# Three instead of two of eight value parts weighted on VectorE, ahead of the keys' last sum, in a two-layer decode kernel

## The chip, the cores and the metric

The kernel runs on one core of a Trainium2 chip. The metric is the device time of one execution in microseconds, as the median of several runs. Before the change it is 2681.38 us (three runs, 2681.13 to 2682.27).

## What is computed

Two decoder layers, each a block of attention over a cache and a gated MLP, for two sequences (B = 2) with one new token each. Both layers use the same weights and the same caches. All numbers are 32-bit floats.

```python
B, Sq, D = 2, 1, 576
H, Sk, Dh = 32, 8192, 128        # k_cache and v_cache: (B, H, Sk, Dh)
Dm, Df = 576, 4608

def _A_ref(x, k_cache, v_cache, wq, wo):
    q = (x @ wq).reshape(B, Sq, H, Dh).transpose(0, 2, 1, 3)
    scores = jnp.einsum("bhqd,bhkd->bhqk", q, k_cache) * (Dh ** -0.5)
    p = _softmax(scores, axis=-1)
    o = jnp.einsum("bhqk,bhkd->bhqd", p, v_cache)
    return o.transpose(0, 2, 1, 3).reshape(B, Sq, H * Dh) @ wo

def _B_ref(x, w_gate, w_up, w_down):
    h = _gelu(jnp.einsum("bsd,df->bsf", x, w_gate)) * jnp.einsum("bsd,df->bsf", x, w_up)
    return jnp.einsum("bsf,fd->bsd", h, w_down)

x = A_x
x = x + _A_ref(_layernorm(x), A_k_cache, A_v_cache, A_wq, A_wo)
x = x + _B_ref(_layernorm(x), B_w_gate, B_w_up, B_w_down)
x = x + _A_ref(_layernorm(x), A_k_cache, A_v_cache, A_wq, A_wo)
x = x + _B_ref(_layernorm(x), B_w_gate, B_w_up, B_w_down)
```

Each cache holds 2 x 32 x 8192 x 128 floats, 268 MB, and is read once in each layer, except for a few pieces that stay on the chip between the layers. With the weights, 1152.4 MB are read.

## The kernel before

**Items.** Attention is cut into items. Most are pairs of heads of one sequence: K of an item is 2 x 8192 rows of 128 floats, laid over 128 partitions as 128 rows each, 64 KB a partition, 8.39 MB in all; V likewise. Such an item has eight *parts* of 16 rows (`JC`). There are 30 pairs and 4 single heads; layer 0 runs through them forwards, layer 1 backwards (`seq`). `i` counts the place in that order, `n = seq[i]` is the item whose keys are multiplied, `p = seq[i - 1]` the one before it, and `f = seq[i - 2]` the one before that.

**Space and transfers.** The tile `space` holds six slots of four parts, used as three places for a whole K or a whole V. All transfers are issued by the SP queue (L168 for the caches) in a planned order: K of item n + 1, then V of item n, and so on. A transfer waits on SP until its place has been freed, and everything behind it waits too. With three places, one transfer moves, one may be queued behind it, and the third place is worked on. A place is free when all of its parts are `done`. In the steady state the place of a K comes free with the keys' last sum (`add_up`), and into it goes the next V; the place of a V comes free with `folded`, and into it goes the next K.

**Keys.** `multiply` (L743, VectorE) forms K times the query in place, 48, 48 and 32 rows at a time (`units`; 6144, 6144 and 4096 elements a partition). The query stands in the PSUM tile `bank`, where TensorE broadcasts it (`query`, L658); it is made one item ahead. GpSimd adds the upper half of each row to the lower (L772), and VectorE sums the 64 remaining (`add_up`, L775). The third sum of an item is left to the start of the next item's code (`ahead`), followed by the maximum (`peak`: L799 on VectorE, and a transpose L801 on TensorE). Then `highest` (L807, L809), `softmax` (two exponentials on ScalarE, L832, into the tile `prz`), `total` and `inverse`.

**Values.** `values` (L913, TensorE) multiplies the weights in `prz` with V, four rows of a part at a time, and adds up in the PSUM tile `acc`. For an item for which `folds` is true (24 in layer 0, 25 in layer 1) it leaves out the last `FOLD` parts. These are done otherwise: `weigh` forms the weights' `share` in PSUM (L875, VectorE; the tile is a part of `bank2`), multiplies the rows of the last parts with it in place (L880, VectorE), and lets GpSimd fold them to four rows by adding halves (L883). `folded` then adds these four rows with one matmul (L891) and frees the parts. `weigh(f)` and `folded(f)` belong to the item two places back, `values` to the item one place back. In every second item `gather` (L927 and L928 on VectorE) and `context` (L936) collect the output of two items.

**The order.** The instructions of each engine run in the order in which `attention` issues them; the loop over `seq` is written out by hand, by places `j` between the three `multiply` of an item. Before the change the start of an item's code reads: last sum and maximum of `p`, `weigh(f)`; then `multiply` 0 and, behind it, `query` of the next item; `folded(f)` comes at `j == 1`, behind `highest`, `softmax`, `total` and `inverse`.

```python
            if first or ahead:
                add_up(p, *units(p)[-1])
                peak(p)
            if f is not None:
                weigh(f)
```

Of the kernel before, what the change touches and what calls it, by code (L numbers as in the profile page):

```python
# [43 lines left out]
END = RING + NPLACE * PLACE  # L44
HELD = 5
SPLIT = (18, 18, 12, 16)
FOLD = 2


class Item:  # L50
# [75 lines left out]
def decode_layers(ctx, tc, x_in, kc, vc, wq, wo, wg, wu, wd, out):  # L126
# [28 lines left out]
    def done(key):  # L155
        arena.free(key)
        pump()

    def part_at(at, n):
        return space[:, at:at + n]  # L160
# [180 lines left out]
    def name(kind, layer, n):  # L341

        return kind, 1 if n in (KEYS_HELD if kind == "k" else VALUES_HELD) else layer, n
# [167 lines left out]
    low = bank2[:, 4 * GH + P + 6:]  # L511
    share = low[:, :FOLD * JC]
    kept = psum1.tile([P, JC, DH], F32, name="kept")
# [93 lines left out]
    def attention(layer):  # L607
# [42 lines left out]
        def query(n):  # L650

            it = ITEMS[n]
            qps.append(qps.pop(0))
            qb[n] = qps[0]
            for i in range(it.heads):
                h, to = it.h + i, slice(i * HALF, i * HALF + P // it.heads)
                c, r = (h // 4) % 4, h // 16 * B + it.b
                nc.tensor.matmul(  # L658
                    qb[n][to, :], pick[32 * c:32 * c + 4, r:r + 1].to_broadcast([4, P // it.heads]),
                    qsb[32 * c:32 * c + 4, (h % 4) * DH:(h % 4 + 1) * DH], start=True, stop=True,  # L660
                )
# [5 lines left out]
        def at_once(n, k):  # L667

            return layer == 1 and n == seq[0] and k in (0, ITEMS[n].parts - 1)

        def units(n):

            if n >= PAIRS or waited(n) or layer == 1 and n == seq[-1]:
                return [(k, 1) for k in range(ITEMS[n].parts)]

            if layer == 1 and n == PAIRS - 2:
                return [(k, 2) for k in range(0, 8, 2)]
            return [(0, 3), (3, 3), (6, 2)]

        def several(n):  # L680
            return units(n)[0][1] > 1
# [92 lines left out]
        def add_up(n, k, m):  # L774
            nc.vector.tensor_reduce(  # L775
                out=S[n][:, base(n, k):base(n, k) + own_rows(n, k, m)], in_=prod.pop((n, k)), axis=AX.X, op=ALU.add
            )
            if layer == 0 and n in KEYS_HELD:
                if n == N - 1 and k >= 2:
                    done(("products", k - 2))  # L780
                return
            key = name("k", layer, n)
            for k in range(k, k + m - 1):
                done((key, k))
            k += m > 1
            if layer == 1 and n == SINGLE[1]:

                if k == 0:
                    ready[key][3] = ready[key][0][:, :JC]
                    nc.scalar.copy(ready[key][3], kept)  # L790
                    return
                k = k % 3
            done((key, k))
            if k == ITEMS[n].parts - 1 or not any(c == key for c, _ in arena.live):
                ready.pop(key)

        def peak(n):
            m = work.tile([P, 1], F32, name="m")
            nc.vector.reduce_max(m, S[n][:, :ITEMS[n].rows], axis=AX.X)  # L799
            mT[n] = small(1, P)  # L800
            nc.tensor.transpose(mT[n], m, ident)  # L801
# [9 lines left out]
        def weights_of(n):  # L811

            if ITEMS[n].heads == 2:
                return prz.rearrange("p a e -> p (a e)")
            return prz[:, n - PAIRS, :]
# [44 lines left out]
        def accumulator(n):  # L860
            return acc[:, (n // B + 1) % 2 if n < PAIRS else (n - PAIRS) // B, :]

        def completes(i):

            return i > 0 and ITEMS[seq[i - 1]].h == ITEMS[seq[i]].h

        def folds(n):

            return (2, 1)[layer] < n < PAIRS - 3

        def weigh(n):

            lo = ITEMS[n].parts - FOLD
            pr = weights_of(n)[:, 8 + 4 * JC * lo:8 + 4 * JC * (lo + FOLD)].rearrange("p (g a e) -> p a g e", a=4, e=4)
            nc.vector.tensor_tensor(  # L875
                out=share.rearrange("p (g e) -> p g e", e=4), in0=pr[:, 0], in1=pr[:, 1], op=ALU.add
            )
            rows = FOLD * JC
            t = part_at(arena.live[name("v", layer, n), lo][0], FOLD * PART).rearrange("p (j d) -> p j d", d=DH)
            nc.vector.tensor_tensor(out=t, in0=t, in1=share.unsqueeze(2).to_broadcast([P, rows, DH]), op=ALU.mult)  # L880
            while rows > 4:
                less = rows // 2 if rows % 8 == 0 else rows - 4
                nc.gpsimd.tensor_tensor(  # L883
                    out=t[:, :rows - less], in0=t[:, :rows - less], in1=t[:, less:rows], op=ALU.add
                )
                rows = less

        def folded(n):

            key, lo = name("v", layer, n), ITEMS[n].parts - FOLD  # L890
            nc.tensor.matmul(  # L891
                accumulator(n)[0:16, :], owner[:, 8 * ITEMS[n].b:8 * ITEMS[n].b + 16],
                part_at(arena.live[key, lo][0], 4 * DH), start=False, stop=completes(seq.index(n)),
            )
            for k in range(lo, lo + FOLD):
                done((key, k))
            ready.pop(key)
# [98 lines left out]
        for i, n in enumerate(seq):  # L996
            last = i == N - 1
            p = seq[i - 1] if i else None

            v = {N - 2: None, N - 1: N - 3}.get(i, i - 1) if layer == 0 else i - 1  # L1000
            f = seq[i - 2] if i > 1 and folds(seq[i - 2]) else None
            a = seq[i - 2] if i > 1 and completes(i - 2) and not (layer == 0 and last) else None

            soon = layer == 1 and i in (1, 4)
            first = layer == 1 and i == 1
            us = units(n)

            ahead = p is not None and several(p)
            if first:
                query(seq[i + 1])  # L1010
            if first or ahead:
                add_up(p, *units(p)[-1])
                peak(p)
            if f is not None:
                weigh(f)
            if first:
                highest(p)
                softmax(p)
            for j, (k, m) in enumerate(us):
                multiply(n, k, m)  # L1020
                if j == 0 and not last and not first and (i or layer == 0):
                    query(seq[i + 1])
                if at_once(n, k) and k == 0:
                    add_up(n, k, m)
                if j == 1 and first:
                    values(v)
                    total(p)
                if j == 0 and p is not None and not first and not ahead:
                    add_up(p, *units(p)[-1])
                    peak(p)  # L1030
                if j == (0 if soon or ahead else 1) and p is not None and not first:
                    highest(p)
                    softmax(p)
                if j == (1 if several(n) else 2) and not first:
                    if p is not None:
                        total(p)
                        inverse(p)
                    if f is not None:
                        folded(f)
                    if a is not None:  # L1040
                        gather(a)
                        if p < PAIRS:
                            context(a)
                    if v is not None and v >= 0:
                        values(v)
                    if a is not None and p >= PAIRS:
                        context(a)
                if j > 0 and (n, us[j - 1][0]) in prod:
                    add_up(n, *us[j - 1])
                if j == 3 and first:  # L1050
                    inverse(p)
                if j == (2 if several(n) else 3) and a is not None and p < PAIRS:
                    divide(a, several(n))
                if j == 1 and late is not None:
                    divide(late)
            late = a if a is not None and p >= PAIRS else None
            if layer == 1 and i == 0:

                nc.vector.scalar_tensor_tensor(qsb, acc[:, 0, :], rstd, qsb, op0=ALU.mult, op1=ALU.add)
# [49 lines left out]
    def mlp(layer):  # L1109
# [106 lines left out]
        if layer == 0:  # L1216
            idle_products(1, 0)

    attention(0)
    mlp(0)  # L1220
    attention(1)
    mlp(1)
    write(nc.scalar)
# [27 lines left out]
```

## Time and profile before

| what | value |
|---|---|
| median of three runs | 2681.38 us |
| lowest and highest run | 2681.13 and 2682.27 us |
| span of the profiled execution | 2681.6 us |
| read from memory | 1152.39 MB, 430 GB/s over the span |
| folded items | 49 |

For the profiled execution the profile gives no time but its span, from the first to the last instruction. On the profile's page a row of digits stands for the span in 40 equal slices, each digit the busy share in tenths. "DMA" among the engines is the mean over the core's 16 DMA engines. In the views of single instructions the columns are start and length in us, engine, line and operation, output and inputs by the program's tile names, and in brackets the idle time before it and what ended this idle time ("releaser"). SPq means the queue of issues on SyncE.

### The profile page before, as it was taken

How to read it: one execution, taken by the hardware profiler on the slowest of the kernel's cores; microseconds unless marked ns; L12 is line 12 of the kernel's file. 1: busy time of each engine (PE TensorE's matmuls, PEld its weight loads, DVE VectorE, ACT ScalarE, POOL GpSimd, SP SyncE). 2: the span in 40 equal slices, each digit the busy share in tenths (PEclk: the TensorE clock that was granted, in tenths of full speed). 3: DMA queues.
4: the chain of work that ended last, by engine and by line, in shares of the span. 5: the costliest groups of instructions: out<-in, count | busy, mean ns of one | idle time of the engine just before them, and what ended most of it. 6: DMA issues, size and time to landing. Idle time of an engine off the chain costs nothing.

```text
span 2681.6 us, 15416 instructions
## 1 busy us (share of the span) xinstructions
PE 885.1 (33%) x6198; PEld 270.4 (10%) x6198; DVE 1992.5 (74%) x907; ACT 165.7 (6%) x792; POOL 1560.5 (58%) x412
## 2 busy tenths in 40 slices
PE   1323332232223232334663323233223323332346
PEld 0000000000000000011221000000000000000022
DVE  4878888888788888867038778878888888888740
ACT  0000000000000000001026000000000000000000
POOL 2546676667666766744028457666766676676620
PEclk8556655665566566566986665566566556655678
DMA  9999999999999999999999999999999999999998
GB/s 422 436 437 427 434 434 431 436 430 435 432 431 433 431 437 433 429 430 427 417 417 426 434 432 432 435 435 430 431 435 433 432 432 435 434 428 434 433 428 378
DMA packets 29344, 1153.41 MB, mean 430 GB/s; under 512 B 3384, under 2 KB 3416, under 8 KB 4184
## 3 DMA queue, kind: packets, MB, share of 16 engines
q1 hardware_dynamic: 29088, 1152.40, 99.7%
q8 instruction: 49, 0.80, 0.1%
q14 instruction: 23, 0.19, 0.0%
q10 hardware_dynamic: 184, 0.02, 0.0%
HBM read 1152.39 MB, written 0.01 MB: 430 GB/s over the span
## 4 chain that ended last, share of the span: by engine, by line
DMA 67%; DVE 20%; PE 8%; POOL 2%; ACT 2%; issue 1%; SPq 0%; POOLq 0%; ACTq 0%; DVEq 0%
DMA space<-in_A_k_cache_dram 60%; DVE space L743 17%; PE acc L891 3%; DMA space<-in_B_w_down_dram 3%; DMA space<-in_B_w_gate_dram 2%; POOL space L772 2%; DVE scores L775 2%; PE bank L658 1%; DMA space<-in_B_w_up_dram 1%; PE bank L809 1%; ACT prz L832 1%; DMA space<-in_A_v_cache_dram 1%; PE bank L845 1%; PE acc L913 0%; PE bank L1210 0%
## 5 line engine op out<-in xcount | busy, mean ns | idle before, releaser
L772 POOL TENSOR_TENSOR space<-space 128x3072 f32<-128x3072 f32 (+4 forms) x221 | 1128.2, 5105 | 461.3 <-DVE space L743 330.9
L743 DVE TENSOR_TENSOR space<-space,bank 128x6144 f32<-128x6144 f32 (+4 forms) x223 | 1111.9, 4987 | 346.1 <-DMA space<-in_A_k_cache_dram 274.6
L775 DVE TENSOR_REDUCE scores<-space 128x48 f32<-128x3072 f32 (+4 forms) x223 | 568.7, 2550 | 93.1 <-POOL space L772 92.9
L913 PE MATMUL acc<-space,prz 128*16 128x512 f32 (+1 forms) x3312 | 513.7, 785 | 353.9 <-DMA space<-in_A_v_cache_dram 342.3
L883 POOL TENSOR_TENSOR space<-space 128x2048 f32<-128x2048 f32 x147 | 398.0, 2708 | 392.6 <-DVE space L880 377.0
L658 PE MATMUL bank<-qsb,few 4*64 4x128 f32 (+1 forms) x256 | 45.5, 433 | 895.0 <-DVE space L743 887.4
L880 DVE TENSOR_TENSOR space<-space,bank 128x4096 f32<-128x4096 f32 x49 | 216.6, 4420 | 1.7
L913 PEld LDWEIGHTS acc<-space,prz 128*16 128x16 f32 (+1 forms) x3312 | 108.7, 117 | 740.3 <-issue 454.0
L824 ACT ACTIVATE nbs<-bank 128x2 f32<-128x2 f32 (+1 forms) x68 | 11.6, 171 | 2012.5 <-PE bank L809 1975.4
L658 PEld LDWEIGHTS bank<-qsb,few 4*64 4x64 f32 (+1 forms) x256 | 20.2, 199 | 914.6 <-DVE space L743 897.9
L580 POOL TENSOR_TENSOR rstd<-ve,few 128x1 f32<-128x1 f32 x4 | 2.2, 551 | 168.3 <-DVE ve L578 168.3
L891 PE MATMUL acc<-space,few 128*16 128x512 f32 x98 | 92.6, 1048 | 0.7 <-POOL space L883 0.7
L801 PE MATMUL bank<-ident,m 128*1 128x128 f32 x68 | 21.1, 310 | 196.5 <-DVE m L799 196.2
L936 PE MATMUL bank<-few,wide 128*32 128x4 f32 (+1 forms) x272 | 20.9, 200 | 170.5 <-DVE wide L928 170.5
L1162 DVE STREAM_TRANSPOSE gu<-acc 128x288 f32<-128x288 f32 x4 | 1.9, 483 | 93.0 <-ACT acc L1160 93.0
L832 ACT ACTIVATE prz<-scores,nbs 64x128 f32<-64x128 f32 (+1 forms) x128 | 50.7, 396 | 11.7 <-POOL prz L822 8.9
L765 ACT ACTIVATE space<-space 128x128 f32<-128x128 f32 x164 | 48.4, 296 | 19.4 <-DVE space L743 16.4
L809 PE MATMUL bank<-m,few 1*128 1x2 f32 (+1 forms) x136 | 38.8, 352 | 26.9 <-DVE m L807 26.9
L584 DVE TENSOR_TENSOR x<-bank,x 128x144 f32<-128x144 f32 x4 | 1.2, 308 | 60.5 <-PE bank L1210 41.5
L927 DVE TENSOR_TENSOR acc<-acc,few 128x512 f32<-128x512 f32 x34 | 23.5, 691 | 26.7 <-PE acc L913 26.7
L936 PEld LDWEIGHTS bank<-few,wide 128*32 128x32 f32 x272 | 19.0, 154 | 216.6 <-issue 211.6
L759 POOL TENSOR_TENSOR space<-space,qs 128x512 f32<-128x512 f32 x23 | 29.2, 1271 | 18.5 <-ACT qs L740 18.5
(106 smaller groups left out, 498.2 us busy)
## 6 DMA issues: line engine op xcount, KB each, us to landing
space<-in_A_v_cache_dram SPq DMA_DIRECT2D x7, 4096.0 KB
space<-in_A_k_cache_dram SPq DMA_DIRECT2D x6, 4096.0 KB
space<-in_B_w_gate_dram SPq DMA_DIRECT2D x9, 1152.0 KB
space<-in_B_w_up_dram SPq DMA_DIRECT2D x9, 1152.0 KB
space<-in_B_w_down_dram SPq DMA_DIRECT2D x8, 1152.0 KB
space<-in_A_wq_dram SPq DMA_DIRECT2D x9, 1024.0 KB
space<-in_A_wo_dram SPq DMA_DIRECT2D x2, 4608.0 KB
space<-in_A_k_cache_dram SPq DMA_DIRECT2D x4, 2048.0 KB
```

The source lines that it names most:

```text
L658: nc.tensor.matmul(qb[n][to, :], pick[32 * c:32 * c + 4, r:r + 1].to_broadcast([4, P // it.heads]), qsb[32 * c:32 * c + 4, (h % 4) * DH:(h ...
L743: nc.vector.tensor_tensor(out=u[:, :r, :], in0=t[:, :r, :], in1=qb[n].unsqueeze(1).to_broadcast([P, r, DH]), op=ALU.mult)
L765: nc.scalar.activation(u[:, j, :], u[:, j, :], AF.Copy, accum_out=S[n][:, base(n, k) + j:base(n, k) + j + 1])
L772: nc.gpsimd.tensor_tensor(out=half, in0=half, in1=u[:, :r, DH // 2:], op=ALU.add)
L775: nc.vector.tensor_reduce(out=S[n][:, base(n, k):base(n, k) + own_rows(n, k, m)], in_=prod.pop((n, k)), axis=AX.X, op=ALU.add)
L809: nc.tensor.matmul(mT[n][:, :heads], ones[0:1, :], m1[:, :heads], start=True, stop=True)
L832: nc.scalar.activation(pr[at, lo:].rearrange("p (g e) -> p g e", e=4)[:, 0:it.rows // 2 * it.heads:2 * it.heads, :], s[at, :it.rows].rearr ...
L880: nc.vector.tensor_tensor(out=t, in0=t, in1=share.unsqueeze(2).to_broadcast([P, rows, DH]), op=ALU.mult)
L883: nc.gpsimd.tensor_tensor(out=t[:, :rows - less], in0=t[:, :rows - less], in1=t[:, less:rows], op=ALU.add)
L891: nc.tensor.matmul(accumulator(n)[0:16, :], owner[:, 8 * ITEMS[n].b:8 * ITEMS[n].b + 16], part_at(arena.live[key, lo][0], 4 * DH), start=F ...
L913: nc.tensor.matmul(accumulator(n)[32 * c:32 * c + m, :], pr[:, at:at + m], t[g // 4][:, g % 4 * 4:g % 4 * 4 + 4, :].rearrange("p j d -> p ...
L936: nc.tensor.matmul(po[lo:lo + 32, i, :c], t[:, i::GH], of[:, :c], start=True, stop=True)
```

## The change

`FOLD` goes from 2 to 3: of the eight parts of a folded item's V, the last three are weighted on VectorE and folded on GpSimd, and TensorE multiplies five. `weigh(f)` is moved from behind the last sum and the maximum of `p` to ahead of them. `folded(f)` is moved from the third place inside the item (behind `highest`, `softmax`, `total`, `inverse`) to right behind the next item's `query`.

```diff
-FOLD = 2
+FOLD = 3
...
             if first:
                 query(seq[i + 1])
+            if f is not None:
+                weigh(f)
             if first or ahead:
                 add_up(p, *units(p)[-1])
                 peak(p)
-            if f is not None:
-                weigh(f)
             if first:
                 highest(p)
                 softmax(p)
@@
                 if j == 0 and not last and not first and (i or layer == 0):
                     query(seq[i + 1])
+                if j == 0 and f is not None:
+                    folded(f)
                 if at_once(n, k) and k == 0:
                     add_up(n, k, m)
@@
                     if p is not None:
                         total(p)
                         inverse(p)
-                    if f is not None:
-                        folded(f)
                     if a is not None:
                         gather(a)
```

On VectorE, around the start of an item in layer 0, the program has before, in this order (`L775` is a sum, `L799` the maximum, `L875` and `L880` the weighing, `L743` a product with the query):

```order
L775 TENSOR_REDUCE scores<-space 128x48
L775 TENSOR_REDUCE scores<-space 128x32
L799 TENSOR_REDUCE m<-scores 128x1
L875 TENSOR_TENSOR bank_124<-prz 128x32
L880 TENSOR_TENSOR space<-space,bank_124 128x4096
L743 TENSOR_TENSOR space<-space,bank 128x6144
```

After the change the same place reads:

```order
L775 TENSOR_REDUCE scores<-space 128x48
L875 TENSOR_TENSOR bank_124<-prz 128x48
L880 TENSOR_TENSOR space<-space,bank_124 128x6144
L775 TENSOR_REDUCE scores<-space 128x32
L799 TENSOR_REDUCE m<-scores 128x1
L743 TENSOR_TENSOR space<-space,bank 128x6144
```

The weighing has become half as long again and stands ahead of the last sum, whose end frees the place for the next V.

On TensorE, from the values of one item to the folded rows of the one before it, the program has before (`L913` values, `L801` the maximum's transpose, `L658` the next query, `L809` the broadcast of the maximum, `L845` the total, `L891` the folded rows):

```order
L913 MATMUL acc_119<-space_69,prz_104 16x512 x24
L801 MATMUL bank2_124<-ident_83,m_1558 1x128
L658 MATMUL bank_122<-qsb_178,few_88 64x128 x2
L809 MATMUL bank2_124<-m1_1570,few_88 128x2
L845 MATMUL bank2_124<-few_88 128x4
L891 MATMUL acc_119<-space_69,few_88 16x512
```

After the change:

```order
L913 MATMUL acc_119<-space_69,prz_104 16x512 x20
L801 MATMUL bank2_124<-ident_83,m_1503 1x128
L658 MATMUL bank_122<-qsb_178,few_88 64x128 x2
L891 MATMUL acc_119<-space_69,few_88 16x512
L809 MATMUL bank2_124<-m1_1512,few_88 128x2
L845 MATMUL bank2_124<-few_88 128x4
```

Four of 24 matmuls of the values are gone, and the folded rows stand two instructions earlier, so that `L809`, on which the softmax waits, is now behind them.

On GpSimd the fold of an item becomes, from

```order
L883 TENSOR_TENSOR space<-space 128x2048
L883 TENSOR_TENSOR space<-space 128x1024
L883 TENSOR_TENSOR space<-space 128x512
L772 TENSOR_TENSOR space<-space 128x48x64 x2
L772 TENSOR_TENSOR space<-space 128x32x64
```

to the following, which has the halves of the next item (`L772`) behind it as before:

```order
L883 TENSOR_TENSOR space<-space 128x3072
L883 TENSOR_TENSOR space<-space 128x1536
L883 TENSOR_TENSOR space<-space 128x512 x2
L772 TENSOR_TENSOR space<-space 128x48x64 x2
L772 TENSOR_TENSOR space<-space 128x32x64
```

The issues on SP are the same, in the same order and into the same places.

## The prediction

> **What bounds the kernel now.** First the page: the span, the engines' busy shares, the DMA row of the 40 slices, the queue that carries the caches, and the chain that ended last.
>
> ```profile
> span 2681.6 us, 15416 instructions
> PE 885.1 (33%) x6198; PEld 270.4 (10%) x6198; DVE 1992.5 (74%) x907; ACT 165.7 (6%) x792; POOL 1560.5 (58%) x412
> DMA  9999999999999999999999999999999999999998
> q1 hardware_dynamic: 29088, 1152.40, 99.7%
> DMA 67%; DVE 20%; PE 8%; POOL 2%; ACT 2%; issue 1%; SPq 0%; POOLq 0%; ACTq 0%; DVEq 0%
> ```
>
> The span (2681.6 us) lies inside the range of the runs (2681.13 to 2682.27, median 2681.38), so sums made against it hold for the runs. No engine is above 74%, while queue q1 has packets moving for 99.7% of the span. The chain's 20% of DVE and 8% of PE are the steps that release the next transfer; they do not yet say that these steps are late. That is read from the steady state. The windows view, over two consecutive items, gives length, then busy time (instructions) of PE, PEld, DVE, ACT and POOL, granted clock, DMA share and GB/s:
>
> ```profile
> 763.26:801.96 38.70, 11.75 (x65) 3.25 (x65) 32.64 (x12) 2.19 (x9) 24.85 (x6) 0.59 1.00 434
> 801.96:840.67 38.71, 11.19 (x59) 2.95 (x59) 31.41 (x11) 1.15 (x5) 27.28 (x8) 0.59 1.00 434
> ```
>
> An item needs one K and one V transfer, 8.39 MB each. Two of them at 434 GB/s are 38.7 us, which is the item's period: 19.35 us a transfer, DMA share 1.00. At that rate the 1152.40 MB of q1 take 2655 us, 99% of the span. **The queue's rate is the bound.** A change of compute can only cost time, by an issue that comes after the queue has run dry, or win back what of the 0.3% of queue idle stems from late issues: at most 8 us.
>
> So the number that decides is the **lead**: from a transfer's issue to the landing of the one in front of it. The timelines of SP (issues), PE (L913 waits for V) and DVE (the first L743 waits for K) give it; columns are start, length, engine and instruction, idle before and its releaser.
>
> ```profile
> 772.92 0.33 SPq L168 DMA_DIRECT2D space<-in_A_k_cache_dram  x1
> 793.13 0.33 SPq L168 DMA_DIRECT2D space<-in_A_v_cache_dram  x1
> 813.50 0.33 SPq L168 DMA_DIRECT2D space<-in_A_k_cache_dram  x1
> 830.58 0.33 SPq L168 DMA_DIRECT2D space<-in_A_v_cache_dram  x1
> ```
>
> ```profile
> 769.87 0.69 PE L658 MATMUL bank<-qsb,few 4*64 4x128 f32 x4 [16.09 <-DVE space L743]
> 782.72 7.84 PE L913 MATMUL acc<-space,prz 128*16 128x512 f32 x48 [3.45 <-DMA space<-in_A_v_cache_dram]
> 808.57 0.69 PE L658 MATMUL bank<-qsb,few 4*64 4x128 f32 x4 [14.73 <-DVE space L743]
> 811.58 1.89 PE L891 MATMUL acc<-space,few 128*16 128x512 f32 x2
> 821.34 7.31 PE L913 MATMUL acc<-space,prz 128*16 128x512 f32 x48 [7.87 <-DMA space<-in_A_v_cache_dram]
> ```
>
> ```profile
> 786.00 3.34 DVE L775 TENSOR_REDUCE scores<-space 128x48 f32<-128x3072 f32 x1
> 790.82 2.29 DVE L775 TENSOR_REDUCE scores<-space 128x32 f32<-128x2048 f32 x1 [1.47 <-POOL space L772]
> 793.87 0.20 DVE L875 TENSOR_TENSOR bank<-prz 128x32 f32<-128x32 f32 x1 [0.45 <-PE bank L801]
> 794.11 4.42 DVE L880 TENSOR_TENSOR space<-space,bank 128x4096 f32<-128x4096 f32 x1
> 801.96 6.55 DVE L743 TENSOR_TENSOR space<-space,bank 128x6144 f32<-128x6144 f32 x1 [3.43 <-DMA space<-in_A_k_cache_dram]
> 823.44 3.35 DVE L775 TENSOR_REDUCE scores<-space 128x48 f32<-128x3072 f32 x1
> 840.67 6.55 DVE L743 TENSOR_TENSOR space<-space,bank 128x6144 f32<-128x6144 f32 x1 [4.71 <-DMA space<-in_A_k_cache_dram]
> ```
>
> V is issued the moment the keys' last sum ends (790.82 + 2.29 = 793.11), K when PE's folded matmul ends (811.58 + 1.89 = 813.47). Leads before: V 801.96 - 793.13 = 8.8 us, then 840.67 - 830.58 = 10.1; K 782.72 - 772.92 = 9.8, then 821.34 - 813.50 = 7.8. Call the item from 763.26 the long one (it has the gather on DVE), the next the short one; they alternate.
>
> **The change part by part.** Durations come from the groups kept apart by shape (count, then busy us, mean ns):
>
> ```profile
> L772 POOL TENSOR_TENSOR space<-space 128x3072 f32<-128x3072 f32 x114 | 763.2, 6695 | 301.1 <-DVE space L743 176.2 <-issue 112.5 <-DVE m L807 12.5
> L743 DVE TENSOR_TENSOR space<-space,bank 128x6144 f32<-128x6144 f32 x114 | 747.2, 6554 | 301.3 <-DMA space<-in_A_k_cache_dram 266.5 <-PE bank L658 34.8
> L883 POOL TENSOR_TENSOR space<-space 128x2048 f32<-128x2048 f32 x49 | 220.3, 4496 | 384.9 <-DVE space L880 377.0 <-issue 7.9
> L880 DVE TENSOR_TENSOR space<-space,bank 128x4096 f32<-128x4096 f32 x49 | 216.6, 4420 | 1.7
> L883 POOL TENSOR_TENSOR space<-space 128x1024 f32<-128x1024 f32 x49 | 115.5, 2356 | 3.8
> L883 POOL TENSOR_TENSOR space<-space 128x512 f32<-128x512 f32 x49 | 62.3, 1271 | 3.9
> ```
>
> *Weigh, 48 rows for 32.* 6144 elements with one operand in PSUM cost 6.55 us (L743 of that size) for 4.42: +2.13 us of DVE an item, +105 us over 49 folded items. No lengthening is taken from L883 or L772 running beside it: L743 takes the same 6.55 at 801.96, beside POOL's fold (row below), as in its mean.
>
> *Fold, 48 rows to 4.* The halvings become 3072, 1536, 512 and 512 elements: 6.70 (L772 of that size), 3.43 (between the 2048 and 1024 rows), 1.27, 1.27, together 12.7 us for 8.1: +4.5 us of POOL an item, +222 over all.
>
> *PE* loses 4 of 24 matmuls of L913, 8 of the 48 instructions that took 7.84 us: -1.3 us an item. It worked off a V that had already landed and nothing waited for its end, so this is worth nothing.
>
> Per period that makes DVE 34.8 and 33.5, POOL at most 31.8 of 38.7 us: nobody becomes the bound by its sum. What counts is the places.
>
> *The weigh ahead of the last sum.* DVE ends its second sum at 786.00 + 3.34 = 789.34. Before, it then waited 1.47 us for POOL's third half, summed 2.29 us, and V went out. Now come the share (0.2), the weigh (6.55, until 796.1) and the sum (POOL is long done, until 798.4). **V goes out 5.3 us later**; in the short item 823.44 + 3.35 + 0.2 + 6.55 + 2.3 = 835.9 for 830.58, also 5.3. Leads for V: 3.5 and 4.8 us. Behind the weigh on DVE stand that sum, the maximum (0.3 us) and the next K's product: DVE is through at 798.7 and 836.2, and K lands at 801.96 and 840.67, so 3.3 and 4.5 us of waiting for K remain. PE's transpose, which waits for the maximum, comes earlier than K too.
>
> *The fold* starts at 796.2, where L880 ended at 798.5 before, and ends at 809.0; the queue on POOL behind it:
>
> ```profile
> 798.61 8.29 POOL L883 TENSOR_TENSOR space<-space 128x2048 f32<-128x2048 f32 x3 [7.83 <-DVE space L880]
> 808.65 6.69 POOL L772 TENSOR_TENSOR space<-space 128x3072 f32<-128x3072 f32 x1 [1.76 <-issue]
> 815.94 6.70 POOL L772 TENSOR_TENSOR space<-space 128x3072 f32<-128x3072 f32 x1 [0.60 <-DVE space L743]
> ```
>
> The first half starts at 809.0 for 808.65 and ends at 815.7; the second cannot start before 815.94 in any case. Cover: 0.2 us; without it the third half and the next sums would slide by that much, inside DVE's 3.3.
>
> *The folded matmul behind the next query.* The query ends at 808.57 + 0.69 = 809.26, after the fold (809.0). L891 runs 809.3 to 811.2 and K goes out there, 2.3 us earlier; after a short item 0.4 earlier. Leads for K: 10.1 and 10.2. The maximum's broadcast (L809) and the exponentials now stand behind L891, some 2 us later, but the values that need them wait for V until 821.34. No SP instruction changes its order.
>
> *The tail.* In the last item of the second layer the fold ends 2.1 us later (weigh from about 2528.1, fold 2534.8 to 2547.5), in front of eight small halves that DVE's sums wait for. The rows there:
>
> ```profile
> 2545.57 1.89 PE L891 MATMUL acc<-space,few 128*16 128x512 f32 x2 [0.68 <-POOL space L883]
> 2576.47 0.18 ACT L832 ACTIVATION_READ_ACCUMULATOR prz<-scores,nbs 64x1 f32 x1
> 2580.51 8.37 PE L913 MATMUL acc<-space,prz 128*16 128x512 f32 x64 [3.22 <-DMA space<-in_A_v_cache_dram]
> ```
>
> The last V leaves with L891's end, 2547.46, now some 2 us later; it lands at 2580.5 and is 19.35 us long, so its lead falls from 13.7 to 11.7. The softmax ends at 2576.65 and slips to 2578.8, still ahead of that landing. Without this cover it would cost up to 2 us, once.
>
> **What lead the queue needs** no row shows. Lower end: nothing. Nearest rows, first the whole time that SP waited at the end for the 4.5 KB store, then a 1 MB weight load whose issue at 1371.08 landed 8.76 us later, 2.4 of them its own, while the queue stayed full:
>
> ```profile
> SPq L1247 <- DMA out_dram<-x: 1.7, 1, 1.7
> 1371.08 8.76 DMA space<-in_A_wq_dram
> 1369.00:1383.00 14.00, 9.03 (x59) 1.81 (x59) 1.30 (x4) 1.11 (x3) 0.88 (x2) 1.00 1.01 401
> ```
>
> So 6.3 us is known to do; that is the upper end, and it would cost (6.3 - 3.5) x 25 + (6.3 - 4.8) x 24 = 106 us. A whole small transfer, waiting included, is over in 1.7. I take the need to be about 2 us, from the small one, since reaching the queue is the same errand for both: 3.5 covers it, and the sum is zero.
>
> The Trainium skill's "DMA: Bandwidth & Descriptors" (Latency and other measured facts) gives 0.6 us to a first byte for this path and up to 2 us of HBM access at high load. By that the need is an estimated 2.6 us, no run here shows it, the sum is still zero, and 0.9 us of lead is left in the long item.
>
> **Rivals.** (1) *The late V starves the queue.* It decides from a need above 3.5 us in the long item. For: the lead there falls by 60%. A stage of this trace shows an issue that came too late, 1440.51, and a queue at 0.93:
>
> ```profile
> 1440.51 0.33 SPq L168 DMA_DIRECT2D space<-in_A_k_cache_dram  x1
> 1438.00:1446.00 8.00, 5.34 (x41) 2.30 (x37) 7.00 (x8) 5.31 (x35) 6.31 (x5) 0.71 0.93 365
> ```
>
> 0.07 x 8.00 = 0.56 us lost. At that price 25 long items give +14 us, 2695; all 49 give +27, 2709; half the price is 2688. Against: 1.7 us. Chance 0.11. (2) *The weigh is held up by POOL*, beside whose third half it now runs. That half ends at 790.8 at the latest, so a weigh that waits for it starts 1.2 us late and leaves a lead of 2.3: near the need of 2, and at a loss of 0.3 us in 25 items 2689. Against: L743's unchanged 6.55. Chance 0.03. (3) *Earlier K issues win back queue idle.* All 8 us of it would give 2673, but the steady state shows 1.00. Chance 0.02. (4) *The weights, V's release and all else stay hidden*, the forecast: 0.84.
>
> On the ceiling of (3), the same page (Where 436 GB/s comes from) puts the ports at 435 GB/s, which the trace's 434 bears out; the same section lets HBM bind a core at about 358, which would make this span 3219 us, and there the measurement decides.
>
> **How the numbers follow.** The likeliest is the queue's time as it was, 2681.4, with 2680 to 2684 as its own range. The high end takes in the mild half of (1) and of (2), 2689; the low end is that of the own range, since (3) has 0.02. 0.2% is 5.4 us, about what a measurement tells from no change: slower 0.13, the cases (1) and (2) less their mildest; faster 0.02; same 0.85.
>
> **What would show it.** Right: L880 at 6.55 us, L883 at 12.7 us an item, V issues 34 to 35 us after their K's product begins for 29 to 30, DVE still waiting 3 to 4 us for K, items of 38.7 us, q1 above 99%. Wrong: items of over 38.8 us; DMA share under 1.00 in the steady state; a V that lands over 19.4 us behind its K (rival 1); L880 over 6.6 us (rival 2). A DVE that no longer waits for K at L743 would overturn the whole sum.

## The result: slower by 1.6%

| | before | after |
|---|---|---|
| median of four runs, us | 2681.45 | 2723.85 |
| lowest and highest, us | 2681.13 to 2682.27 | 2719.57 to 2731.77 |
| span of the profiled execution, us | 2681.6 | 2717.9 |
| ratio, 95% interval | | 1.0162, 1.015 to 1.0174 |

The changed kernel takes 42 us longer, where no change was forecast and 2689 was the range's upper end. The page of the profile after, in the lines that were read first before (span, engines, the DMA row of the 40 slices, the queue of the caches, the chain that ended last):

```profile
span 2717.9 us, 14657 instructions
PE 851.9 (31%) x5806; PEld 260.1 (10%) x5806; DVE 2155.4 (79%) x907; ACT 165.5 (6%) x792; POOL 1779.1 (65%) x461
DMA  9999999999999999999999999999999999999999
q1 hardware_dynamic: 29088, 1152.40, 99.1%
DMA 55%; DVE 27%; POOL 10%; PE 5%; issue 2%; ACT 1%; POOLq 0%; SPq 0%; DVEq 0%; ACTq 0%
```

These lines hardly tell that 36 us of span were added. The row of digits reads full in every slice, and q1's 99.1% would even do for the prediction's "above 99%". What shows is the chain: DMA holds 55% of it instead of 67%, DVE 27% for 20, POOL 10% for 2. Late releases now set the end where the queue's rate did. The loss itself stands in the rate, in the windows view of the 800 us from 300 to 1100, before and then after (the last three columns are granted clock, DMA share, GB/s):

```profile
300.00:1100.00 800.00, 235.30 (x1304) 64.80 (x1304) 663.29 (x238) 35.66 (x149) 539.92 (x124) 0.59 1.00 433
```

```profile
300.00:1100.00 800.00, 217.75 (x1088) 59.10 (x1088) 716.76 (x233) 34.60 (x145) 620.66 (x144) 0.59 0.99 425
```

8 of 433 GB/s over these 800 us are 15 us of transfer that did not move. A single item needn't show it: some of the periods below are still 38.7 us.

**The places.** The issues on SP and the work on DVE over two items after (start, length, instruction, and in brackets the wait ahead of it and what ended it):

```profile
769.13 0.33 SPq L168 DMA_DIRECT2D space<-in_A_v_cache_dram  x1
782.01 0.33 SPq L168 DMA_DIRECT2D space<-in_A_k_cache_dram  x1
809.18 0.33 SPq L168 DMA_DIRECT2D space<-in_A_v_cache_dram  x1
821.89 0.33 SPq L168 DMA_DIRECT2D space<-in_A_k_cache_dram  x1
847.80 0.33 SPq L168 DMA_DIRECT2D space<-in_A_v_cache_dram  x1
```

```profile
772.86 6.55 DVE L743 TENSOR_TENSOR space<-space,bank 128x6144 f32<-128x6144 f32 x1 [3.44 <-DMA space<-in_A_k_cache_dram]
...
798.86 1.50 DVE L875 TENSOR_TENSOR bank<-prz 128x48 f32<-128x48 f32 x1
800.40 6.55 DVE L880 TENSOR_TENSOR space<-space,bank 128x6144 f32<-128x6144 f32 x1
806.87 2.28 DVE L775 TENSOR_REDUCE scores<-space 128x32 f32<-128x2048 f32 x1
...
811.58 6.55 DVE L743 TENSOR_TENSOR space<-space,bank 128x6144 f32<-128x6144 f32 x1 [2.10 <-DMA space<-in_A_k_cache_dram]
...
826.61 3.35 DVE L775 TENSOR_REDUCE scores<-space 128x48 f32<-128x3072 f32 x1 [1.05 <-POOL space L772]
...
837.47 1.52 DVE L875 TENSOR_TENSOR bank<-prz 128x48 f32<-128x48 f32 x1
...
850.30 6.55 DVE L743 TENSOR_TENSOR space<-space,bank 128x6144 f32<-128x6144 f32 x1 [2.20 <-DMA space<-in_A_k_cache_dram]
```

V goes out 36.3 us behind the start of its K's product in the long item (809.18 - 772.86) and 36.2 in the short one (847.80 - 811.58), where 34 to 35 were forecast. The leads are 2.4 us (811.58 - 809.18) and 2.5 (850.30 - 847.80), for 3.5 and 4.8. Two things took the difference: L875, put at 0.2 us, took 1.5; and in the short item the first sum waited 1.05 us for POOL. POOL's timeline at these places:

```profile
795.76 4.54 POOL L772 TENSOR_TENSOR space<-space 128x2048 f32<-128x2048 f32 x1 [2.23 <-DVE space L743]
807.04 12.88 POOL L883 TENSOR_TENSOR space<-space 128x3072 f32<-128x3072 f32 x4 [6.74 <-DVE space L880]
819.88 13.36 POOL L772 TENSOR_TENSOR space<-space 128x3072 f32<-128x3072 f32 x2
```

The third half ends at 795.76 + 4.54 = 800.30, and L875 at 798.86 + 1.50 = 800.36. The fold ends 8.3 us behind the start of the next K's product (819.92 - 811.58), where before it was 4.9 (806.90 - 801.96); the halves follow without a gap, where before there was one of 1.76 us, so the first half starts 1.6 us later.

The groups apart by shape, after, and L875's of before (count, busy us, mean ns, idle time ahead):

```profile
L883 POOL TENSOR_TENSOR space<-space 128x3072 f32<-128x3072 f32 x49 | 326.5, 6662 | 330.3 <-DVE space L880 323.5 <-issue 6.8
L880 DVE TENSOR_TENSOR space<-space,bank 128x6144 f32<-128x6144 f32 x49 | 321.1, 6554 | 1.7
L883 POOL TENSOR_TENSOR space<-space 128x1536 f32<-128x1536 f32 x49 | 168.6, 3442 | 3.8
L883 POOL TENSOR_TENSOR space<-space 128x512 f32<-128x512 f32 x98 | 124.2, 1268 | 7.7
...
L875 DVE TENSOR_TENSOR bank<-prz 128x48 f32<-128x48 f32 x49 | 74.5, 1520 | 0.0
```

```profile
L875 DVE TENSOR_TENSOR bank<-prz 128x32 f32<-128x32 f32 x49 | 9.8, 201 | 23.4 <-PE bank L801 23.4
```

The weigh (6.55 us) and the fold (12.6 us by these rows) are what the prediction took. L875 isn't: half as many elements more, and 7.6 times the time.

### The profile page after: what moved, and what is told of

Read it like the earlier page. It is cut to its first block, busy times and chain, and to the rows that moved or that the text cites. A ratio compares the mean times of both kernels' runs of the same rounds, so it can differ in the third digit from the quotient of the medians.

```text
span 2717.9 us, 14657 instructions
## 1 busy us (share of the span) xinstructions
PE 851.9 (31%) x5806; PEld 260.1 (10%) x5806; DVE 2155.4 (79%) x907; ACT 165.5 (6%) x792; POOL 1779.1 (65%) x461
## 3 DMA queue, kind: packets, MB, share of 16 engines
q1 hardware_dynamic: 29088, 1152.40, 99.1%
## 4 chain that ended last, share of the span: by engine, by line
DMA 55%; DVE 27%; POOL 10%; PE 5%; issue 2%; ACT 1%; POOLq 0%; SPq 0%; DVEq 0%; ACTq 0%
DMA space<-in_A_k_cache_dram 47%; DVE space L743 17%; POOL space L883 7%; DVE scores L775 5%; DVE space L880 3%; POOL space L772 3%; DMA space<-in_B_w_down_dram 2%; PE acc L891 2%; DMA space<-in_B_w_gate_dram 2%; DMA space<-in_A_v_cache_dram 1%; DMA space<-in_B_w_up_dram 1%; PE bank L658 1%; DVE bank L875 1%; DMA space<-in_A_wo_dram 1%; PE acc L913 1%
## 5 line engine op out<-in xcount | busy, mean ns | idle before, releaser
L743 DVE TENSOR_TENSOR space<-space,bank 128x6144 f32<-128x6144 f32 (+4 forms) x223 | 1111.9, 4987 | 302.8 <-DMA space<-in_A_k_cache_dram 231.8
L772 POOL TENSOR_TENSOR space<-space 128x3072 f32<-128x3072 f32 (+4 forms) x221 | 1127.0, 5104 | 335.2 <-DVE space L743 306.5
L883 POOL TENSOR_TENSOR space<-space 128x3072 f32<-128x3072 f32 x196 | 619.3, 3160 | 341.8 <-DVE space L880 323.5
L775 DVE TENSOR_REDUCE scores<-space 128x48 f32<-128x3072 f32 (+4 forms) x223 | 568.9, 2551 | 38.3 <-POOL space L772 38.1
L913 PE MATMUL acc<-space,prz 128*16 128x512 f32 (+1 forms) x2920 | 472.5, 812 | 358.5 <-DMA space<-in_A_v_cache_dram 345.7
L880 DVE TENSOR_TENSOR space<-space,bank 128x6144 f32<-128x6144 f32 x49 | 321.1, 6554 | 1.7
L658 PE MATMUL bank<-qsb,few 4*64 4x128 f32 (+1 forms) x256 | 46.0, 436 | 603.2 <-DVE space L743 595.5
L801 PE MATMUL bank<-ident,m 128*1 128x128 f32 x68 | 24.4, 359 | 545.0 <-DVE m L799 544.9
L913 PEld LDWEIGHTS acc<-space,prz 128*16 128x16 f32 (+1 forms) x2920 | 98.6, 120 | 675.5 <-issue 424.3
L891 PE MATMUL acc<-space,few 128*16 128x512 f32 x98 | 92.5, 1048 | 27.3 <-POOL space L883 27.1
L658 PEld LDWEIGHTS bank<-qsb,few 4*64 4x64 f32 (+1 forms) x256 | 20.6, 201 | 626.3 <-DVE space L743 609.5
L875 DVE TENSOR_TENSOR bank<-prz 128x48 f32<-128x48 f32 x49 | 74.5, 1520 | 0.0
L801 PEld LDWEIGHTS bank<-ident,m 128*1 128x1 f32 x68 | 5.4, 79 | 600.9 <-DVE m L799 302.4
L809 PE MATMUL bank<-m,few 1*128 1x2 f32 (+1 forms) x136 | 39.2, 356 | 15.0 <-DVE m L807 15.0
L809 PEld LDWEIGHTS bank<-m,few 1*128 1x128 f32 x136 | 33.4, 304 | 102.8 <-issue 85.1
```

The source lines that it names most:

```text
L658: nc.tensor.matmul(qb[n][to, :], pick[32 * c:32 * c + 4, r:r + 1].to_broadcast([4, P // it.heads]), qsb[32 * c:32 * c + 4, (h % 4) * DH:(h ...
L743: nc.vector.tensor_tensor(out=u[:, :r, :], in0=t[:, :r, :], in1=qb[n].unsqueeze(1).to_broadcast([P, r, DH]), op=ALU.mult)
L772: nc.gpsimd.tensor_tensor(out=half, in0=half, in1=u[:, :r, DH // 2:], op=ALU.add)
L775: nc.vector.tensor_reduce(out=S[n][:, base(n, k):base(n, k) + own_rows(n, k, m)], in_=prod.pop((n, k)), axis=AX.X, op=ALU.add)
L809: nc.tensor.matmul(mT[n][:, :heads], ones[0:1, :], m1[:, :heads], start=True, stop=True)
L875: nc.vector.tensor_tensor(out=share.rearrange("p (g e) -> p g e", e=4), in0=pr[:, 0], in1=pr[:, 1], op=ALU.add)
```

## Experiments

The leading theory: the time goes with V's lead, and L875, held by GpSimd, takes the lead below what the queue needs, then thought to be 3 to 4 us. Its rivals: the lead is short enough to cost even with a share of 0.2 us, or the cause isn't V's lead at all but the longer fold or the folded rows' new place. Each expectation says what they give for its kernel. "Lead" is always from V's issue to DVE's start on the K in front. Each part of the change was tried alone.

### The share alone, ahead of the last sum (e4_share_ahead)

The kernel before, with L875 alone moved in front of the last sum.

```diff
-        def weigh(n):
+        def shares(n):
...
+            if f is not None:
+                shares(f)
             if first or ahead:
                 add_up(p, *units(p)[-1])
```

> The kernel before, with the share of two parts alone moved ahead of the keys' last sum; the weigh stays behind it. GpSimd's third half is then still running, and VectorE has to wait for that half anyway before the last sum. Theory A: the share takes 1.2 to 1.4 us instead of 0.20, ends with GpSimd's third half, and the time stays at 2681 to 2683 us. Theory B': the share was long because it has 48 elements or another place: then it takes 0.2 us here.

Measured: 2681.13 us, ratio 1.0 (0.999 to 1.0011). L875 by its line (ns: least, median, most), then DVE's and POOL's timelines:

```profile
L875 DVE TENSOR_TENSOR bank<-prz x49: 1491/1575/1592, 206.1 to 2525.7; 128x32 f32<-128x32 f32 x49
```

```profile
789.35 1.57 DVE L875 TENSOR_TENSOR bank<-prz 128x32 f32<-128x32 f32 x1
790.90 2.29 DVE L775 TENSOR_REDUCE scores<-space 128x32 f32<-128x2048 f32 x1
```

```profile
786.31 4.55 POOL L772 TENSOR_TENSOR space<-space 128x2048 f32<-128x2048 f32 x1 [2.30 <-DVE space L743]
```

The same 32 columns that took 0.201 us take 1.58 when a half runs beside them, and end 0.06 us behind it (786.31 + 4.55 = 790.86). It costs nothing here, because the sum behind it waits for that half anyway.

### The change with a share that GpSimd doesn't hold (e1_share_psum)

L875 adds two operands that both lie in SBUF (`prz`). L743 and L880, which ran beside POOL at their usual time, have one of theirs in PSUM. Here ScalarE first copies one of L875's operands to PSUM; all else is the change.

```diff
+            other = low[:, FOLD * JC:2 * FOLD * JC].rearrange("p (g e) -> p g e", e=4)
+            nc.scalar.copy(other, pr[:, 1])
             nc.vector.tensor_tensor(
-                out=share.rearrange("p (g e) -> p g e", e=4), in0=pr[:, 0], in1=pr[:, 1], op=ALU.add
+                out=share.rearrange("p (g e) -> p g e", e=4), in0=pr[:, 0], in1=other, op=ALU.add
             )
```

> The changed kernel with one edit: ScalarE copies one half of the weights to PSUM, so that the share (L875 in the changed kernel) reads one operand from SBUF and one from PSUM instead of two from SBUF. Theory A (the share was held until GpSimd's third half ended, 1.3 us in every folded item, and the queue needs 3 to 4 us of lead): the share takes 0.2 to 0.3 us, V goes out 1.3 us earlier in the long items and about 2 us earlier in the short ones, leads of 3.7 and about 4.7 us, and nearly all of the 40 us go: 2682 to 2692 us. Theory B (the share's length does not matter, the longer weigh and fold on VectorE and GpSimd set the pace): 2712 us or more, though the share is short.

Measured: 2701.17 us, ratio 1.0075 (1.006 to 1.009), between the two. DVE's timeline, and SP's:

```profile
796.86 0.20 DVE L877 TENSOR_TENSOR bank<-prz,bank 128x48 f32<-128x48 f32 x1
797.10 6.55 DVE L882 TENSOR_TENSOR space<-space,bank 128x6144 f32<-128x6144 f32 x1
...
809.56 6.55 DVE L743 TENSOR_TENSOR space<-space,bank 128x6144 f32<-128x6144 f32 x1 [3.39 <-DMA space<-in_A_k_cache_dram]
```

```profile
805.87 0.33 SPq L168 DMA_DIRECT2D space<-in_A_v_cache_dram  x1
```

The share is back at 0.20 us with the half beside it (POOL's L772 runs from 793.76 to 798.31), so the second SBUF operand is what held it. V's lead is 3.69 us here (809.56 - 805.87), and DVE waits 3.39 us for K: this is the kernel that the prediction described, with its leads and its waits. It loses 20 us. So holding explains about half (2723.85 - 2701.17 = 23); the other half comes with leads that were thought to be enough.

### The delay alone (e5_hold_0, e5_hold_4)

To have the lead by itself: the kernel before, in its old order and size, but V's issue waits for a copy of one element that stands behind the weigh; in the second kernel four small maxima stand ahead of that copy.

```diff
-        def add_up(n, k, m):
+        def add_up(n, k, m, hold=False):
...
+            if not hold:
+                release(n, k, m)
...
+            nc.vector.tensor_copy(junk, keys(n, k, m)[:, m * JC - 1, DH - 1:])
...
+            if held:
+                for _ in range(0):
+                    nc.vector.reduce_max(junk, S[p][:, :ITEMS[p].rows], axis=AX.X)
+                look(p, *units(p)[-1])
+                release(p, *units(p)[-1])
```

> The kernel before, with its two weighted parts and its order, but the next V is issued only after the weigh (a copy of one element of the keys' products, behind the weigh, is what V waits for). VectorE and GpSimd do the same work as before. V goes out about 5.5 us later: leads of 3.3 us in the long and 4.6 us in the short items. Theory A (the queue needs 3 to 4 us of lead, and only the late V costs time): 2682 to 2692 us. The need of 2 us that the prediction took: 2681.5 us. Theory B (the pace is set by VectorE and GpSimd): 2681.5 us.

> As the run before, with four small maxima (0.29 us each) between the weigh and the copy that V waits for: V goes out 1.2 us later still, leads of 2.1 and 3.4 us. Theory A: about 1.5 us lost in each of 25 long items and 0.3 in the short ones, 2705 to 2730 us, about what the change cost. The need of 2 us: 2682 us. Theory B: 2682 us, since VectorE still waits 1 to 2 us for every K.

Measured: 2707.76 us, ratio 1.0099 (1.0084 to 1.0114), and 2726.12 us, 1.0167 (1.015 to 1.0184). The first is above what was expected, and far from what the prediction's need of 2 us gives, which is no loss: at these leads a delay of V's issue by itself costs 27 us, with nothing of the change in the kernel. The second lies where it was expected. In the first (e5_hold_0) DVE still waits for K at such a place, as it should:

```profile
807.25 0.15 DVE L788 COPY junk<-space 128x1 f32<-128x1 f32 x1
810.75 6.55 DVE L744 TENSOR_TENSOR space<-space,bank 128x6144 f32<-128x6144 f32 x1 [3.35 <-DMA space<-in_A_k_cache_dram]
```

Long and short items alternate in this first kernel, and the loss with them. Between 300 and 1110 us, ten V issues have leads of 3.2 to 3.6 us, and the period that begins with the K in front is 39.86 us on average; nine have leads of 5.0 to 6.4, and there it is 38.77.

The same was then read from nine of the traces (before, after, e1, e2, both e5, e4, e6 and e7), every period in that stretch put by the lead ahead of it. The second column is the number of periods, the third their mean less 38.70 us:

```
lead us      periods   lost us
1.9 to 2.7     17       1.55
2.7 to 3.2      9       0.58
3.2 to 3.8     29       0.98
3.8 to 4.6     18       0.61
4.6 to 5.3     18       0.18
5.3 to 6.0     22       0.17
6.0 to 8.5     20       0.05
over 8.5       38       0.08
```

Below some 4.6 us the queue loses 0.6 to 1.6 us a time; above 6 the loss is at the level of before itself. Single periods scatter (38.7 to 41.4 at the shortest leads). **The need of lead by K's landing is about 5 us, not 2.**

What happens there shows in windows of one packet's time (64 KB, 2.42 us; a packet counts in the window in which it starts). After, around V's issue at 809.18; then before, up to the landing at 801.96:

```profile
807.70:810.12 2.42, 0.37 (x1) 0.08 (x1) 1.74 (x2) 0.00 (x0) 2.42 (x1) 0.50 0.25 108
810.12:812.54 2.42, 0.00 (x0) 0.00 (x0) 0.96 (x1) 0.00 (x0) 2.42 (x1) 0.50 1.25 433
```

```profile
797.50:799.92 2.42, 0.00 (x0) 0.00 (x0) 1.03 (x1) 0.00 (x0) 1.31 (x1) 0.50 1.00 433
799.92:802.34 2.42, 0.00 (x0) 0.00 (x0) 0.38 (x1) 0.00 (x0) 2.42 (x1) 0.50 1.00 433
```

K lands at 811.58. A full queue starts 16 packets in each window; here a quarter of that start between 807.70 and 810.12. So three quarters of the 16 engines had begun their last packet of K before 807.70, were done with it by 810.12, and had nothing next. The landing that DVE sees is that of the last engine; the others run dry ahead of it.

The trace's records of single packets give the moments, since each engine closes its share of a transfer with a write of 4 bytes. At this place twelve engines end K between 809.41 and 810.00, the last at 811.04, and DVE starts at 811.58. V's first packet starts at 810.16, 0.98 us behind its issue, and fourteen of V's sixteen first packets take 2.85 to 3.34 us instead of 2.42. So a late issue costs in two ways, by engines that stand idle and by slow first packets; from 300 to 1110 us, compared with before, the changed kernel loses 6.1 and 7.9 us of each engine's time by them. The engine that ended last loses nothing here, which is why a single period need not show the loss.

Counted from V's issue to the moment when the first engine ends K, the V issues of the same nine traces sort more cleanly. The third column is what an engine loses around the handover, idle time and time above 2.42 us a packet, as the mean of the 16:

```
lead us      V issues   lost us
below 0         16        1.81
0 to 1.0        24        1.02
1.0 to 1.8      34        0.47
1.8 to 2.5      16        0.08
over 2.5        90        0.01
```

By this count about 2 us is enough. The need is 5 us by the landing because the engines' ends of one transfer lie 0.4 to 3.8 us apart in these traces. The V issue at 847.80 shows it: its lead by the landing is 2.5 us, no more than the 2.4 at 809.18, but K's engines end within 0.35 us of each other there (849.57 to 849.92), and an engine loses under 0.1 us instead of 1.1.

What pulls the engines apart are single packets of two other queues, which the page after lists as

```profile
q8 instruction: 45, 0.74, 0.1%
q14 instruction: 23, 0.19, 0.0%
```

Between 300 and 1110 us before, a packet of q8, with the slower cache packet behind it, sets a single engine back by 1.6 us (10 packets), one of q14 by 0.7 to 1.0 us (6 packets). Over 27 handovers without such a packet the distance between the first and the last engine changes by 0.01 us at most. A late issue brings the engines together (0.35 us apart at the end of V, behind the issue at 809.18), and the next such packets pull them apart again (from 0.59 to 1.64 us over the transfer with the q8 packet at 873.91).

### Order without size, held and not held (e2_order_only, e7_order_share_psum)

The changed order with `FOLD` = 2, as it is and with the share of e1.

```diff
-FOLD = 3
+FOLD = 2
```

> The changed kernel with two weighted parts again: the weigh ahead of the last sum and the folded rows behind the next query, but 4.4 us of weigh and 8.1 us of fold. Theory A: the share is held by GpSimd's third half (1.5 us for 0.2), V goes out about 4.3 us later than before, leads of 4.4 and 5.7 us by the landing of the K in front; by the runs with held issues that is just short of enough in the long items, 2682 to 2690 us. If the size of the fold is what costs, 2681.5 us.

> Two weighted parts, the changed kernel's order, and the share with one operand in PSUM. Theory A: the share takes 0.2 us, V goes out 3 us later than before, leads of 5.7 and 7 us, which the held issues show to be enough: 2680 to 2683 us. If moving the weigh costs in itself: 2685 us or more.

Measured: 2691.39 us, ratio 1.0045 (1.0028 to 1.0061), just above what was expected, and 2681.35, ratio 1.0 (0.9991 to 1.0009). With e1 and the change itself this makes a square; in brackets the lowest and the mean lead between 300 and 1110 us:

| | share not held | share held |
|---|---|---|
| 32 rows, new order | 2681.35 (5.8; 6.5) | 2691.39 (4.4; 5.4) |
| 48 rows, new order | 2701.17 (3.7; 4.8) | 2723.85 (2.4; 3.4) |

In this square the time goes with the lead, whatever shortens it: holding costs 10 us from a lead of 5.8 and 23 from 3.7. Moving the weigh is free only while the lead stays near 6 us.

### The folded rows at their old place (e6_fold_old_place)

The change, with `folded(f)` back behind `inverse(p)`.

> The changed kernel with the folded rows back at their old place behind the softmax's broadcast. Theory A: K goes out 0.5 to 2.5 us later, with leads of still 7 us or more, V as in the changed kernel: 2716 to 2730 us, the same as the change. If the move of the folded rows carried part of the cost, over 5 us away from the changed kernel.

Measured: 2718.25 us, ratio 1.0138 (1.0123 to 1.0153), beside 1.0162 (1.015 to 1.0174). The move of L891 carries nothing of the loss that was looked for; a few us in its disfavour are at the edge of what these intervals tell.

### Size without order (e3_size_only)

The kernel before with `FOLD` = 3 alone, to see what the new order is good for.

> The kernel before with three weighted parts and nothing moved: sum, maximum, share, weigh, and the folded rows at their old place. Here one ring closes: GpSimd's three halves, the last sum 2.3, maximum and transpose 0.7, share 0.2, weigh 6.55, fold 12.8 and again the halves 18.0 us, together 40.5 to 41 us for an item of 38.7. Theory A with this ring: about 2 us an item, 2765 to 2800 us, worse than the whole change. If only the late V counts: V goes out some 3 us later than before, leads over 5 us, 2682 to 2690 us.

Measured: 2821.07 us, ratio 1.0522 (1.0506 to 1.0538), above the expected range. DVE's timeline:

```profile
762.47 6.55 DVE L743 TENSOR_TENSOR space<-space,bank 128x6144 f32<-128x6144 f32 x1
...
782.27 3.35 DVE L775 TENSOR_REDUCE scores<-space 128x48 f32<-128x3072 f32 x1 [5.82 <-POOL space L772]
...
804.44 6.55 DVE L743 TENSOR_TENSOR space<-space,bank 128x6144 f32<-128x6144 f32 x1
```

The share takes 0.22 us here with 48 columns, as no half runs beside it at its old place. The product at 762.47 no longer waits for K, and the period is 41.97 us (804.44 - 762.47), though neither DVE nor POOL has that much work. It is a ring: the fold holds POOL, the first half comes behind it, DVE's sums wait for that half (5.82 us), and behind the sums stand the last sum, the maximum and the weigh, which the next fold waits for. Sums of busy time by engine, as the prediction made them, don't contain it. In the changed order the last sum and the maximum stand behind the weigh, out of the ring, so the order is needed for the size; the ring is then just short enough to show as 1.05 us in short items.

### The weigh cut in two (e8_split_16_32, e9_split_32_16)

To win the lead back: the changed kernel with e1's share and 16 (then 32) of the 48 rows weighted ahead of the last sum, the rest behind the maximum.

```diff
             if f is not None:
-                weigh(f)
+                weigh_first(f)
             if first or ahead:
                 add_up(p, *units(p)[-1])
                 peak(p)
+            if f is not None:
+                weigh(f)
```

> Three weighted parts, the changed kernel's place for the folded rows, the share with one operand in PSUM, and the weigh cut in two: 16 rows (2.3 us) ahead of the keys' last sum, 32 rows (4.4 us) behind it. Theory A: V goes out about 1 us later than in the kernel before, leads of 7.7 us and more, so the queue never waits for V; but the ring of GpSimd and VectorE (fold 12.9, first half 6.7, sum and product 7.7, third half 4.6, last sum 2.3, maximum 0.3, rest of the weigh 4.4, handing over 0.3) is 39.2 us for an item of 38.7: 0.5 us an item, 2695 to 2712 us. If only the lead of V counted: 2681 to 2684 us.

> As the run beside it, with 32 rows (4.4 us) ahead of the last sum and 16 (2.3 us) behind it. Theory A: V goes out 3 us later than in the kernel before, leads of 5.7 and 7 us, the same as in the run with two parts in the changed order and the short share, which lost nothing; the ring is 37.0 us, under 38.7: 2680 to 2685 us with the same three parts weighted and folded. If three parts are too much for VectorE or GpSimd in any order: 2690 us or more.

Measured: 2754.29 us, ratio 1.0272 (1.0257 to 1.0287), and 2754.59, 1.0273 (1.0255 to 1.029). Both expectations missed, by 42 and 70 us above the upper end of their ranges, with the same time. DVE of the second:

```profile
772.65 0.20 DVE L877 TENSOR_TENSOR bank<-prz,bank 128x48 f32<-128x48 f32 x1
...
780.29 2.29 DVE L888 TENSOR_TENSOR space<-space,bank 128x2048 f32<-128x2048 f32 x1 [0.47 <-PE bank L801]
782.84 6.55 DVE L743 TENSOR_TENSOR space<-space,bank 128x6144 f32<-128x6144 f32 x1 [0.27 <-DMA space<-in_A_k_cache_dram]
...
802.22 3.35 DVE L775 TENSOR_REDUCE scores<-space 128x48 f32<-128x3072 f32 x1 [3.25 <-POOL space L772]
...
809.82 3.35 DVE L775 TENSOR_REDUCE scores<-space 128x48 f32<-128x3072 f32 x1
813.08 0.20 DVE L877 TENSOR_TENSOR bank<-prz,bank 128x48 f32<-128x48 f32 x1
813.32 4.42 DVE L888 TENSOR_TENSOR space<-space,bank 128x4096 f32<-128x4096 f32 x1
```

The period is 40.4 us (813.08 - 772.65), and K is hardly waited for: the ring again. The fold still needs the second piece of the weigh, so all of it, the last sum, the maximum and its transpose lie in the ring wherever the cut is. The working behind the two expectations (39.2 and 37.0 us) led the ring through POOL's third half, 4.6 us; the longer way goes through DVE's second sum, the share and the first piece of the weigh, 3.35 + 0.20 + 4.42 = 8.0 us in the second kernel and 5.8 in the first, which makes 40.4 of both. No version was found that beats the kernel before.

## Why the prediction was wrong

- **What lead the queue needs: this step failed first.** It was taken as 2 us, from the 1.7 us of a small store, with 6.3 as the end known to do. The runs show about 5 us. About 2 us would do if the first engine's end were meant; but the lead was counted to the landing, which is the last engine's, and the 16 engines do not end together. That the number fits the other count may be luck: the store goes by another queue, and no run shows that its errand is the same. The share that was not held, with the leads as predicted, loses 20 us on this term alone; the delay alone, 27. The 2.6 us estimated from the Trainium skill's "DMA: Bandwidth & Descriptors" (Latency and other measured facts) contains only the way to a first byte. No run bears it out as a lead counted to the landing, where 3.3 us were not enough.
- **The share at 0.2 us: failed, it took 1.5.** That is the other 23 us. Rival (2) had the place and the size (a start 1.2 us late, behind POOL's third half), but on the weigh, and was set aside with L743's unchanged 6.55. L743 has an operand in PSUM and says nothing on L875, which has two in SBUF. The Trainium skill states this in "SBUF — State Buffer" (SBUF: two separate sides): VectorE and GpSimd share a pair of ports as an exclusive lock, which a VectorE instruction with two SBUF inputs contends for against a GpSimd instruction that reads SBUF; the later one stands until the other is over. The trace agrees: 0.06 us after the half's end, in e4 and after alike.
- **Rival (1) was what happened**, and its point of decision (a need above 3.5 us in the long item) was right. It had been put at 0.11 against the 1.7 us of the store, and its price of 0.56 us a late issue was too small: below 4.6 us of lead the runs show 0.6 to 1.6.
- **The cover of 0.2 us on POOL** was gone at once. The slide was forecast to stay inside DVE's wait for K; it does delay V, by 1.05 us in short items, since V's issue hangs on the sums that wait for POOL.
- Right were the bound, the weigh (6.55), the fold (12.88 in the timeline for 12.7), L891 ahead of the softmax at no cost that shows, and PE's fewer matmuls worth nothing.

Added up by the square, the new size at its leads costs 20 us and the held share 23; the medians are 42.4 apart. Still open is why the first packets after a late issue are slow; no experiment separates this from the idle time.

## What to carry to other kernels

Where a queue's rate is the bound, count the lead to the moment when the first DMA engine runs dry, not to the landing that the consumer sees; here, with 8 MB transfers, 2 us by that count were enough, and 5 to 6 us by the landing. Before an instruction is moved on VectorE, look at what GpSimd runs at its new place and where its operands lie: two SBUF operands behind a 4.5 us half cost 1.3 us, one in PSUM nothing. And add up the rings of engines that wait for each other, instruction by instruction: no sum of busy time by engine showed the periods of 40.4 and 42 us.

## What the hardware showed that was not expected

A small VectorE add of two SBUF operands stood for 1.3 us until GpSimd's instruction ended (0.20 to 1.5 us, in 49 of 49 cases), while large ones with an operand in PSUM ran beside GpSimd at 6.55 us as ever. The 16 DMA engines ended one 8 MB transfer up to 3.8 us apart, set back one at a time by single packets of the instruction queues, so that a queue with its next transfer issued 2.4 us ahead of the landing had three quarters of its engines idle for part of that time. The first packets after such a late issue took up to 3.34 us instead of 2.42.
